# Five loads of E issued by GpSimd, the end of the cosine on VectorE, and the identity on the sync queue

## The chip, the cores and the metric

The kernel runs on one core of a Trainium2 chip. The core has a matrix engine (TensorE, PE in the profile, with its weight loads as PEld), a vector engine (VectorE, DVE), a scalar engine (ScalarE, ACT), GpSimd (POOL) and a sync engine (SP) that only issues DMAs. Each engine runs its own instructions in order and waits on semaphores for the others. SP, ACT and POOL can all issue DMAs. The metric is the device time of one execution in microseconds, the median over several runs. Less is better.

## What is computed

Two layers act on the same normalised input, and their results are added to it: a state-space convolution (`_A_ref`) and a gated feed-forward layer (`_B_ref`).

Between K and the return stands a causal convolution y of each channel of u with K, by FFT over 4096 points.

```python
def _A_ref(u, A_re, A_im, B_re, B_im, C_re, C_im, log_dt, Dskip):
    dt = jnp.exp(log_dt)[:, None]
    logdA = dt * (A_re + 1j * A_im)
    dB = dt * (B_re + 1j * B_im)
    P = jnp.exp(logdA[:, :, None] * l[None, None, :])     # l = 0 .. 2047
    K = jnp.einsum("dn,dnl,dn->dl", Cc, P, dB).real
    ...
    return y + u * Dskip[None, None, :]

def _B_ref(x, w_gate, w_up, w_down):
    h = _sigmoid(x @ w_gate) * (x @ w_up)
    return h @ w_down

x = A_u                                                    # 1 x 2048 x 512, bf16
xn = _layernorm(x, axis=-1)
return x + _A_ref(xn, ...) + _B_ref(xn, w_gate, w_up, w_down)
```

## The kernel before, in words

The convolution is done with a factored Fourier transform whose parts are matrix products. First the parameters are turned into `exp(dt*A)`, as a real and an imaginary part: its magnitude comes from an exponential, its angle from a sine and a cosine. The angle, reduced to turns, is in `w0`. ACT computes `sh`, the sine of half the angle, and `sn`, the sine of the angle, and then squares `sh` and scales it to 1 - 2 `sh`², which is the cosine (`f_sin`, L620 to L624). DVE multiplies both by the magnitude (`f_w0`, L631 and L632). From there a ladder of eleven squarings (L666 on ACT, L673 and L675 on DVE) gives the powers 1, 2, 4 and so on up to 1024, and complex products of these (`cmul`, L734 to L740, and `squares`, L789 to L795) fill two tables of powers, G and H. The product of G and H on PE (L820) gives the convolution kernel K, which goes through DRAM (`k_scr`) into the layout `kT`.

The second stage of the transform runs over two halves of the channels, p = 0 and p = 1, and over 8 units u in each, in the order that `UNITS` gives. For each unit:

- L881 transforms the unit's part of the input on PE, and ACT or DVE evicts it into `xx`. A copy with its halves of partitions swapped is made beside it, for p = 0 and for the units of `SWD` by four swap DMAs of 32 partitions on SP (`big<-big 32x1024`), else by four copies on DVE (L894).
- L907 transforms K by the constant table E of the unit: 320 KB, `es` in the code and `big<-c_E` in the profile. It is ten matmuls, evicted into `kb` by ACT.
- DVE multiplies the two spectra (L912 and L916), and L931 on PE transforms the product back. The result is evicted and stored in DRAM (`v_scr`).

The tables E have three buffers (pool `es`). In the first half all 8 are loaded; those of the units 4, 6 and 7 (`SHARED`) stay in their buffers for the second half, so that the second half loads five. A load waits until the matmuls that last read its buffer are done. PE works on the second half's units as: two kept ones, the third kept one, and then the five loaded ones. L907, L881 and L931 of all units share two PSUM pairs (pool `s`).

The feed-forward layer fills PE in between: gate (L1042), up (L1067) and down (L1119) products in four groups of 512 tokens, with sigmoids on ACT (L1055, L1058), copies of the up product on ACT (L1082), and products on DVE (L1087, L1092). What it needs of the input is normalised by L537 to L549. The first four tiles of 128 tokens are transposed on PE with the identity (`ident`, L559); the others go through DRAM. At the end L993 adds the last stage of the transform, L1017 and L1139 on DVE add everything up, and the result is stored.

The order of all work is written out by hand. Each operation gets a number in the order in which the code adds it, with an engine; `ORDER` lists the numbers, and each engine executes its operations in that order. So an operation's place in its engine's queue is its place in `ORDER`, whatever engine it has. Ahead of everything else SP loads the first four x tiles (128 KB each), then parameters and weights; ACT loads the identity, behind a small operation (`o_held`, L459) that runs after ACT's first table load. GpSimd (POOL) does small arithmetic and, late, six loads of x that are accumulated into SBUF (`facc`, L1156, 256 KB each). All other DMAs stand in SP's queue, but for a few on ACT.

Of the kernel before, what the change touches and what calls it, by code (L numbers as in the profile page):

```python
# [69 lines left out]
KB = 1024  # L70
# [114 lines left out]
def _consts():  # L185
# [136 lines left out]
def kernel(  # L322
# [116 lines left out]
    def load(q, dst, src, nbytes, deps=(), pkt=2048, hv=0.5):  # L439
        lp[0] += 0.01  # L440
        return dma(q, dst, src, deps=deps, prio=lp[0], pkt=pkt, hv=hv)(nbytes)
# [767 lines left out]
```

## Time and profile before

| what | time |
|---|---|
| median of 3 runs | 213.71 us (213.4 to 214.21) |
| time of the profiled execution | 215.62 us |
| its span, first to last instruction | 213.8 us |
| PE busy | 204.4 us (96%) |
| DVE busy | 195.5 us (91%) |
| ACT busy | 171.5 us (80%) |
| POOL busy | 16.8 us (8%) |

The profile is one execution. A timeline row gives start, duration, engine, line of the kernel, operation, what it writes and reads with shapes, how many instructions are merged in it, and in square brackets how long the engine stood idle before it and what ended that. An engine name with q (SPq, POOLq) is its sequencer or its DMA issues. A windows row gives each engine's busy time in a stretch, the granted PE clock in it, the share of the time that the 16 DMA engines were busy, and their GB/s. A chain row gives start, duration and what worked; the next row in time is what it released. Durations overlap a little: two equal DVE rows of 0.68 us can follow each other by 0.60.

### The profile page before, as it was taken

The numbers are of one execution on the slowest core, as the hardware profiler recorded it, in microseconds if no ns is written. First come the engines' busy times: TensorE is split into PE (matmuls) and PEld (weight loads), VectorE is DVE, ScalarE is ACT, GpSimd is POOL, SyncE is SP. The second block draws the span as 40 slices with busy tenths as digits, with TensorE's granted clock in tenths as the row PEclk, the third lists the DMA queues.
The fourth block names the chain that finished last, engine by engine and source line by source line (L and its number), as shares of the span: only waits on it lengthen the run. The fifth ranks groups of instructions, "written<-read, shape, count | busy, mean of one in ns | idle before, by whom it ended". The sixth has DMA issues, their size and how long they took to land.

```text
span 213.8 us, 4897 instructions
## 1 busy us (share of the span) xinstructions
PE 204.4 (96%) x1856; PEld 102.4 (48%) x1856; DVE 195.5 (91%) x412; ACT 171.5 (80%) x274; POOL 16.8 (8%) x30
## 2 busy tenths in 40 slices
PE   7898999999999999999999999999999979999992
PEld 2653444444444454445437464544653636644571
DVE  3889999999999999999999999999997979994583
ACT  3599999999999999988799998877968777891000
POOL 1003006200820000110000000011000000000000
PEclk9999999999999999999999999999999999999998
DMA  5999379101791457897575778787585569989644
GB/s 169 310 395 364 126 171 311 55 6 38 244 165 46 147 167 249 202 208 189 115 219 143 218 208 251 196 237 156 126 224 161 145 188 321 312 236 296 213 172 172
DMA packets 51465, 42.07 MB, mean 197 GB/s; under 512 B 16545, under 2 KB 44978, under 8 KB 51250
## 3 DMA queue, kind: packets, MB, share of 16 engines
q1 hardware_dynamic: 49650, 39.72, 61.7%
q0 software_dynamic: 864, 1.57, 5.1%
q10 hardware_dynamic: 928, 0.47, 0.8%
q8 instruction: 14, 0.23, 0.4%
q14 instruction: 9, 0.07, 0.1%
HBM read 24.44 MB, written 12.85 MB: 174 GB/s over the span
## 4 chain that ended last, share of the span: by engine, by line
DVE 61%; PE 20%; DMA 6%; ACT 5%; issue 4%; SPq 1%; DVEq 0%; ACTq 0%
DVE big L735 10%; DVE big L734 10%; DVE big L740 5%; DVE big L739 5%; PE bank L1119 4%; DVE hT_sb L1087 4%; PE bank L1042 4%; PE pair L931 3%; DVE big L673 3%; DVE big L675 3%; DVE big L912 3%; PE pair L907 3%; DVE hT_sb L1092 3%; PE bank L1067 3%; DVE stats L537 2%
## 5 line engine op out<-in xcount | busy, mean ns | idle before, releaser
L291 ACT ACTIVATE big<-pair 128x1024 bf16<-128x1024 f32 x62 | 64.3, 1065 | 9.1 <-PE pair L881 1.7
L1067 PE MATMUL bank<-xnT,wu_sb 128*128 128x512 bf16 x224 | 53.6, 379 | 0.1
L1119 PE MATMUL bank<-wd_sb,hT_sb 128*128 128x512 bf16 (+1 forms) x238 | 50.4, 367 | 0.0
L1042 PE MATMUL bank<-xnT,wg_sb 128*128 128x512 bf16 (+1 forms) x200 | 46.8, 371 | 1.0 <-ACT hT_sb L1055 0.9
L1042 PEld LDWEIGHTS <-wg_sb 128*128 128x128 bf16 x240 | 22.4, 98 | 26.1 <-issue 4.7
L1119 PEld LDWEIGHTS <-hT_sb 128*128 128x128 bf16 x238 | 22.5, 98 | 25.0 <-issue 1.6
L1067 PEld LDWEIGHTS <-wu_sb 128*128 128x128 bf16 x224 | 20.9, 98 | 25.0 <-issue 2.9
L1055 ACT ACTIVATE hT_sb<-bank 128x512 bf16<-128x512 f32 x48 | 29.2, 682 | 0.4 <-PE bank L1042 0.4
L734 DVE TENSOR_TENSOR big<-big 128x1024 bf16<-128x1024 bf16 (+4 forms) x40 | 26.7, 668 | 0.1
L1082 ACT ACTIVATE us_sb<-bank 128x512 bf16<-128x512 f32 x40 | 26.0, 680 | 0.9 <-DVE hT_sb L1087 0.7
L735 DVE TENSOR_TENSOR big<-big 128x1024 bf16<-128x1024 bf16 (+4 forms) x40 | 26.6, 665 | 0.0
L907 PE MATMUL pair<-big 128*128 128x256 bf16 x160 | 19.5, 273 | 2.1 <-DMA big<-c_E 1.5
L912 DVE TENSOR_TENSOR big<-big 128x2048 bf16<-128x2048 bf16 x16 | 19.5, 1220 | 1.2 <-DMA big<-big 1.1
L907 PEld LDWEIGHTS <-big 128*128 128x128 bf16 x160 | 15.3, 98 | 6.8 <-DMA big<-c_E 1.8
L789 ACT ACTIVATE sq_sb<-big 128x256 bf16<-128x256 bf16 (+2 forms) x20 | 14.4, 722 | 3.7 <-DVE big L740 3.3
L739 DVE TENSOR_TENSOR big<-big 128x512 bf16<-128x512 bf16 (+4 forms) x40 | 16.5, 412 | 0.1
L740 DVE TENSOR_TENSOR big<-big 128x512 bf16<-128x512 bf16 (+4 forms) x40 | 16.5, 412 | 0.0
L1087 DVE TENSOR_TENSOR hT_sb<-hT_sb,us_sb 128x1024 bf16<-128x1024 bf16 x20 | 13.6, 680 | 0.0
L666 ACT ACTIVATE big<-big 128x1024 f32<-128x1024 f32 x11 | 13.3, 1211 | 0.0
L931 PE MATMUL pair<-big 64*64 64x512 bf16 (+1 forms) x256 | 13.1, 327 | 0.1
L660 ACT ACTIVATE big<-big 128x512 bf16<-128x512 f32 x20 | 12.7, 754 | 0.0
L291 ACT ACTIVATE big<-big 128x256 bf16<-128x256 bf16 x25 | 11.2, 510 | 0.5 <-PE pair L820 0.5
(99 smaller groups left out, 216.8 us busy)
## 6 DMA issues: line engine op xcount, KB each, us to landing
big<-c_E SPq DMA_DIRECT2D x13, 320.0 KB, 4.1
z_scr<-big SPq DMA_DIRECT2D x16, 256.0 KB, 3.5
big<-z_scr SPq DMA_DIRECT2D x16, 256.0 KB, 3.9
v_scr<-big SPq DMA_DIRECT2D x16, 256.0 KB, 3.8
big<-big SPq DMA_DIRECT2D x44, 64.0 KB, 2.7
wu_sb<-in_B_w_up_dram SPq DMA_DIRECT2D x2, 896.0 KB, 9.4
wd_sb<-in_B_w_down_dram SPq DMA_DIRECT2D x1, 1792.0 KB, 9.9
out_dram<-big SPq DMA_DIRECT2D x7, 256.0 KB, 2.2
```

The costliest lines, as they stand in the source:

```text
L291: nc.scalar.activation(out=get(out), in_=get(in_), func=ACT.Identity)
L734: V.tensor_tensor(out=wide(outp), in0=wide(lo), in1=mre, op=ALU.mult)
L735: V.tensor_tensor(out=wide(tb()), in0=wide(lo), in1=mim, op=ALU.mult)
L739: V.tensor_tensor(out=outp[:, :, 0], in0=outp[:, :, 0], in1=tb()[:, :, 1], op=opr)
L740: V.tensor_tensor(out=outp[:, :, 1], in0=outp[:, :, 1], in1=tb()[:, :, 0], op=opi)
L907: T.matmul(two(sk)[:, o:o + DW], es()[:, g, kt, :], kTv[p][:, :, kt, :], start=kt in (0, NKT - 1), stop=kt >= NKT - 2)
L912: V.tensor_tensor(out=pp().rearrange("p q h m -> p (q h) m"), in0=xx().rearrange("p q h m -> p (q h) m"), in1=kb()[:, 0:2 * DW].unsqueeze( ...
L1042: T.matmul(bank(sl, k % 2)[:, c0:c1], w[:, kt, k * 128:(k + 1) * 128], xnT[:, grp, kt, c0:c1], start=(kt == 0), stop=(kt == KT - 1))
L1055: S.activation(out=hT_sb[:, hs.idx, k % 2, :], in_=bank(sl), func=ACT.Sigmoid)
L1067: T.matmul(bank(sl), wu_sb[:, kt, k * 128:(k + 1) * 128], xnT[:, grp, kt, :], start=(kt == 0), stop=(kt == KT - 1))
L1082: eus.append(pl.add("ACT", 0.48, lambda sl=sl, us=us, kk=kk: S.activation(out=us_sb[:, us.idx, kk % 2, :], in_=bank(sl), func=ACT.Identity ...
L1119: T.matmul(bank(po)[:, 0:c[1] - c[0]], hT_sb[:, hts[k // 2].idx, k % 2, jj * 128:(jj + 1) * 128], wd_sb[:, k, c[0]:c[1]], start=first and ...
```

## The change

It has three parts.

The identity is loaded by SP, third in its queue, behind the second x tile. `o_held` is gone, so ACT has neither that operation nor the DMA. The first rows of SP's queue, as a difference (each row is a run of equal DMAs):

```order
-L1205 UNCONDITIONAL_BRANCH
-L430 DMA big<-in_A_u_dram 128x512 x4
+L1207 UNCONDITIONAL_BRANCH
+L430 DMA big<-in_A_u_dram 128x512 x2
+L430 DMA ident<-c_ident 128x128
+L430 DMA big<-in_A_u_dram 128x512 x2
 L430 DMA big<-in_A_par_dram 128x1536
```

Tiles 3 and 4 of x, the parameters and the weights behind them stand one DMA later.

The square and the scaling of the cosine leave ACT and become a new operation on DVE, `f_cos`. In DVE's queue, where the parameters are worked out, there stood before (statistics of the input, then `f_w0`, then the end of the statistics):

```order
L616 SCALAR_TENSOR_TENSOR big<-big 128x512
L537 BN_STATS stats<-big 128x6 x4
L631 TENSOR_TENSOR big<-big 128x512
L632 TENSOR_TENSOR big<-big 128x512
L538 BN_AGGR mvb<-stats 128x2 x2
```

With the change there stands, in the same place (the line numbers move by one or two):

```order
L615 SCALAR_TENSOR_TENSOR big<-big 128x512
L536 BN_STATS stats<-big 128x6 x4
L625 TENSOR_TENSOR big<-big 128x512
L626 TENSOR_SCALAR big<-big 128x512
L633 TENSOR_TENSOR big<-big 128x512
L634 TENSOR_TENSOR big<-big 128x512
L537 BN_AGGR mvb<-stats 128x2 x2
```

L625 and L626 are new, between the statistics and `f_w0`.

The five loads of E of the second half are issued by GpSimd instead of SP. SP's queue in that part of the program, as a difference (swaps, small loads, stores and reloads stand around them):

```order
 L430 DMA big<-big 32x1024
 L430 DMA big<-in_A_u_dram 4x512
-L430 DMA big<-c_E 128x1280
 L430 DMA big<-big 32x1024 x2
-L430 DMA big<-c_E 128x1280
 L430 DMA xnT<-v_scr_101 128x2048
-L430 DMA big<-c_E 128x1280
 L430 DMA v_scr_104<-big 128x4x256
-L430 DMA big<-c_E 128x1280
```

The fifth stood further down, behind the next two stores and a reload. GpSimd's queue at its end is now, behind two fills of a table:

```order
L771 MEMSET big 128x64x2
L1158 DMA glu_sb<-in_A_u_dram 128x1024 x4
L1158 DMA big<-in_A_u_dram 128x1024 x2
L430 DMA big<-c_E 128x1280 x5
L1207 UNCONDITIONAL_BRANCH
```

The five follow its six accumulating loads of x and nothing follows them. Nothing else changes its place on any engine.

The diff, its table cut to the first line:

```diff
 ORDER = [
-    0, 1, 2, 3, 5, 4, 6, 16, 13, 8, 12, 15, 7, 22, 25, 27, 26, 28, 29, 35, 30, 31, 37, 32, 24, 36, 38, 39, 34, 40,
+    0, 1, 5, 2, 3, 4, 15, 12, 7, 11, 14, 6, 21, 24, 26, 25, 27, 28, 34, 29, 30, 36, 31, 23, 35, 37, 38, 33, 39, 40,
...
-    o_held = pl.add("ACT", 0.2, lambda: S.activation(out=ident[:, 127:128], in_=one[:], func=ACT.Identity), (), 0)
     l_pa = load("SP", par[:, 0:3, :], A_par[:, 0:3, :], 384 * KB, pkt=3072)
-    l_id = load("ACT", ident[:], cten["ident"].ap(), 32 * KB, deps=[o_held])
+    l_id = load("SP", ident[:], cten["ident"].ap(), 32 * KB)
...
     def f_sin():
         S.activation(out=pt_["sh"], in_=pt_["w0"], func=ACT.Sin, scale=PI_S)
         S.activation(out=pt_["sn"], in_=pt_["w0"], func=ACT.Sin, scale=2.0 * PI_S)
-        S.activation(out=pt_["sh"], in_=pt_["sh"], func=ACT.Square)
-        S.activation(out=pt_["sh"], in_=pt_["sh"], func=ACT.Identity, scale=-2.0, bias=one[:])
-    q5 = pl.add("ACT", 2.38, f_sin, [q3, q4], PR, tab="sin")
+    q5 = pl.add("ACT", 1.22, f_sin, [q3, q4], PR, tab="sin")
+
+    def f_cos():
+        V.tensor_tensor(out=pt_["sh"], in0=pt_["sh"], in1=pt_["sh"], op=ALU.mult)
+        V.tensor_scalar(out=pt_["sh"], in0=pt_["sh"], scalar1=-2.0, scalar2=1.0, op0=ALU.mult, op1=ALU.add)
+    q5b = pl.add("DVE", 1.1, f_cos, [q5], PR)
...
-    w0_op = cur_op = pl.add("DVE", 1.25, f_w0, [q5], PR)
+    w0_op = cur_op = pl.add("DVE", 1.25, f_w0, [q5b], PR)
...
-                le = dma("SP", es, cten["E"].ap()[u], deps=w_use[0], prio=QP - 0.5, acq=[esl], pkt=2560, hv=0.9)(320 * KB)
+                le = dma("POOL" if p else "SP", es, cten["E"].ap()[u], deps=w_use[0], prio=QP - 0.5, acq=[esl], pkt=2560, hv=0.9)(320 * KB)
```

28 rows, old and new, of the table ORDER are left out of this document.

## The prediction

> **What bounds the kernel now.** I read the chain that ended last first: by engine it is mostly VectorE (DVE), then TensorE (PE).
>
> ```profile
> DVE 61%; PE 20%; DMA 6%; ACT 5%; issue 4%; SPq 1%; DVEq 0%; ACTq 0%
> ```
>
> Then the busy times by stretch, cut where the chain changes hands.
>
> ```profile
> core 0: us, PE busy (x) PEld busy (x) DVE busy (x) ACT busy (x) POOL busy (x), PEclk, DMA share, GB/s
> 20.00:150.00 130.00, 129.76 (x1134) 60.80 (x1132) 129.44 (x296) 122.31 (x207) 13.98 (x18) 1.00 0.63 171
> 165.00:175.00 10.00, 7.97 (x70) 4.66 (x69) 8.28 (x16) 8.23 (x10) 0.00 (x0) 1.00 0.56 141
> 175.00:193.00 18.00, 17.92 (x192) 10.17 (x191) 17.72 (x31) 14.47 (x18) 0.00 (x0) 1.00 0.93 289
> ```
>
> The reader is to see three things. From 20 to 150 us PE and DVE are both full: PE has 0.24 us of idle time in 130, DVE 0.56. From 165 to 175 us nobody is full: PE stands still for 2.03 of 10 us. From 175 to 193 us PE and DVE are full again. So a microsecond counts if it is added to or taken from DVE before 150 us, or taken from the hole at 165 to 175 us.
>
> Which of the two full engines leads at 150 us is told by the chain there, in order of time:
>
> ```profile
> 148.46 0.36 DVE big L740
> ...
> 149.46 1.01 ACT big L291
> ...
> 150.51 2.34 PE pair L907 x20
> ```
>
> DVE releases an ACT copy, which releases PE's matmuls of L907. PE in turn is only just idle there, so the two lead almost together, and DVE by a hair. What keeps the hole open is a load of the table E:
>
> ```profile
> 169.84 4.58 DMA big<-c_E
> ...
> 174.47 1.27 PE pair L907 x10
> ```
>
> **The sine and cosine: ACT to DVE.** ACT now does table load, two sines, a square and a scaling in a row. These are its rows from the timeline, with start, duration, line and operation:
>
> ```profile
> 12.40 0.63 ACT L621 ACTIVATE big<-big 128x512 f32<-128x512 f32 x1
> 12.94 0.61 ACT L622 ACTIVATE big<-big 128x512 f32<-128x512 f32 x1
> 13.46 0.61 ACT L623 ACTIVATE big<-big 128x512 f32<-128x512 f32 x1
> 14.10 0.72 ACT L624 ACTIVATE big<-big,one 128x512 f32<-128x512 f32 x1
> 14.84 1.28 ACT L1055 ACT_TABLE_LOAD   x1
> ```
>
> L623 and L624 go, so the sigmoid's table load can start at about 13.5 instead of 14.84: ACT is ahead by 1.3 us. DVE's side of the same place:
>
> ```profile
> 10.51 0.43 DVE L615 TENSOR_SCALAR big<-big 128x512 f32<-128x512 f32 x1
> ...
> 11.84 2.47 DVE L537 BATCH_NORM_STATS2 stats<-big 128x6 f32<-128x512 bf16 x4 [0.18 <-DMA big<-in_A_u_dram]
> ...
> 14.86 0.69 DVE L631 TENSOR_TENSOR big<-big 128x512 f32<-128x512 f32 x1 [0.55 <-ACT big L624]
> ```
>
> DVE finishes four statistics at 14.31 and then waits 0.55 us for ACT. The new square is a tensor-tensor of the shape of L631 (0.69 us), the new scaling a tensor-scalar of the shape of L615 (0.43 us). The first sine is ready at 13.0, so DVE starts the square at 14.31 without waiting. It ends at 15.00, the scaling at about 15.45, and L631 starts at about 15.47 instead of 14.86. **That is 0.6 us more on DVE**, 1.1 us of work less 0.5 us of wait that it fills. Of this up to 0.56 us can be swallowed in the idle time that DVE has between 20 and 150 us, if that idle time is spent waiting for ACT or PE, which run earlier now. It is many pieces of a few hundredths, so I take 0.1 us of it: **+0.5 us at 150 us**, with bounds 0 and +0.6. What ACT gains, and the wait of PE for the first sigmoid, are costed at nothing: DVE releases PE at 150.5 us however far ahead PE is.
>
> **The identity on the sync queue.** Before, it waits behind ACT's first table load:
>
> ```profile
> 0.73 1.82 SPq L430 DMA_DIRECT2D big<-in_A_u_dram  x4
> ...
> 5.60 0.74 DVE L549 TENSOR_SCALAR big<-big,mv,ln_ri_f 128x512 bf16<-128x512 bf16 x2
> ...
> 6.57 0.90 PE L559 MATMUL pair<-ident,big 128*128 128x128 bf16 x8 [0.66 <-DMA ident<-c_ident]
> ...
> 8.20 0.42 PEld L1042 LDWEIGHTS <-wg_sb 128*128 128x128 bf16 x4 [0.36 <-DMA wg_sb<-in_B_w_gate_dram]
> ```
>
> An issue on SP costs 0.45 us (1.82 over 4), so the identity is issued at about 1.64 instead of 2.26 and no longer ends the wait. But L559 also needs the scaled x, which ends at 6.34, so at most 0.2 us is won there. Against it, x tiles 3 and 4, the parameters and the first weights are issued 0.45 us later. PE's next step waits for weights that land at about 8.2, and the same bytes stand in the queue ahead of them as before, so I expect no shift from the bytes; if issue time decides, it is 0.45 us. DVE's four statistics at 11.84 wait for a load too, so nothing won before reaches 14.31. I take 0, with bounds -0.2 and +0.45.
>
> **The five E loads on GpSimd.** PE's rows in the hole:
>
> ```profile
> 166.15 2.36 PE L907 MATMUL pair<-big 128*128 128x256 bf16 x20 [0.56 <-ACT big L291]
> ...
> 169.65 1.27 PE L907 MATMUL pair<-big 128*128 128x256 bf16 x10
> ...
> 172.59 0.41 PE L881 MATMUL pair<-big,m 64*64 64x512 bf16 x4
> 174.47 1.27 PE L907 MATMUL pair<-big 128*128 128x256 bf16 x10 [1.47 <-DMA big<-c_E]
> ```
>
> There are three E buffers. The first of the five loads reuses the one that the first half of the row at 166.15 reads, free at about 167.4 (ten matmuls take 1.27). SP issues the load only at 169.84, because swaps, small loads and two stores stand ahead of it in its queue. GpSimd has nothing in its queue after its last accumulating load, which is the nearest row for its price:
>
> ```profile
> 147.65 0.87 POOL L1156 DMA_DIRECT2D big<-in_A_u_dram  x1 [4.57 <-ACT big L291]
> ...
> L1156 POOL DMA_DIRECT2D glu_sb<-in_A_u_dram x4: 866/970/1209, 57.9 to 94.3; - x4
> ...
> DMA to landing us min/median/max: 4.2/5.0/5.5
> ```
>
> Those are 256 KB loads; the E load has 320 KB, another 0.2 us at the 289 GB/s of the windows row. From 167.4 it lands at 167.4 + 5.0 + 0.2 = 172.6, bounds 171.8 and 173.1. PE is ready for it at 173.0, so the wait of 1.47 us goes. Loads two and three come free at 168.6 and 170.9 and land about 174 and 176, ahead of their matmuls; four and five are freed by the matmuls of one and two and keep the distance they have now.
>
> What is late next is DVE, with ACT between:
>
> ```profile
> 173.23 0.69 DVE L916 TENSOR_TENSOR big<-big 128x1024 bf16<-128x1024 bf16 x1
> 173.97 0.59 ACT L1082 ACTIVATE us_sb<-bank 128x512 bf16<-128x512 f32 x1
> ...
> 174.99 1.22 DVE L912 TENSOR_TENSOR big<-big 128x2048 bf16<-128x2048 bf16 x1 [1.07 <-DMA big<-big]
> 175.82 1.94 ACT L291 ACTIVATE big<-pair 128x1024 bf16<-128x1024 f32 x2 [1.26 <-issue]
> ...
> 176.88 1.23 DVE L912 TENSOR_TENSOR big<-big 128x2048 bf16<-128x2048 bf16 x1
> ```
>
> The L912 at 176.88 is the product that uses E load one. From there DVE is full to 193 us, so **its start is what the tail gains**. With L907 at 173.0 to 174.2, ACT evicts at 174.5 to 175.45. But before it DVE has another L912, held 1.07 us by a swap on SP:
>
> ```profile
> 170.26 2.71 SPq L430 DMA_DIRECT2D big<-big  x2
> ```
>
> These two swaps stand right behind the E load. Without it the pair moves up by about 0.4 us and has 320 KB less ahead of it in its queue, which at 289 GB/s is 1.1 us; I take a landing at 174.0 instead of 174.95. Then the first L912 runs 173.95 to 175.1, L916 to 175.75, and the second L912 starts at 175.75 instead of 176.88: **-1.1 us**. Bounds: -1.47 if DVE takes no part, -0.1 if the swap lands no earlier (then L912 starts at 176.8).
>
> One rule speaks against GpSimd here. Row first: the copies beside which the first load would be issued.
>
> ```profile
> 166.73 1.71 DVE L894 COPY big<-big 32x1024 bf16<-32x1024 bf16 x4
> ```
>
> GpSimd's 0.87 us at 147.65 lay beside tensor-tensor work on DVE, never beside such copies. If the issue waits for the copies to end at 168.44, load one lands at 173.65, its eviction ends at 175.95, and the tail gains 0.9 instead of 1.1 us. The Trainium skill, page "SBUF — State Buffer", section "SBUF: two separate sides", says just this: a DMA issued by GpSimd has its descriptors written through ports that a DVE copy in a two-port mode locks for its whole duration. By that rule the sum is -0.4 instead of -0.6; no run here shows it yet.
>
> **Sum.** +0.5 (cosine on DVE) + 0 (identity) - 1.1 (E loads) = **-0.6 us**. The durations come from the profiled execution, whose span is 213.8 us and whose time is 215.62; there the sum gives a span of 213.2. The median of the unprofiled runs is 213.71, so I predict **213.1 us**.
>
> **Rivals.**
> First, DVE doesn't pay (212.4 us). If the 0.56 us of DVE's idle time before 150 us is mostly waiting for ACT or PE, ACT's 1.3 us of lead fills it and the front costs 0; the tail gives between 1.1 and 1.47, say 1.3. For it: PE is as full as DVE. Against it: the chain runs along DVE, and the idle time is in crumbs.
> Second, the swap takes the place of the E load (214.0 us). PE gets its table in time, but DVE still waits for the swap until near 175, and the tail gains 0.2 only; with +0.5 in front that is +0.3. For it: a swap of 64 KB waited long although it is small. Against: it stood behind the load that moves away.
> Third, slower: GpSimd is held by DVE (215.1 us). One GpSimd instruction shows how far it can be stretched (the last row is PE's use of loads four and five):
>
> ```profile
> 33.93 0.29 POOL L497 TENSOR_SCALAR ln_ve_b<-mvb 128x4 bf16<-128x4 bf16 x1 [14.20 <-DVE mvb L538]
> 53.73 2.41 POOL L497 TENSOR_SCALAR ln_ve_b<-mvb 128x4 bf16<-128x4 bf16 x1 [14.70 <-DVE mvb L538]
> ...
> 184.53 2.35 PE L907 MATMUL pair<-big 128*128 128x256 bf16 x20
> ```
>
> The same instruction takes 2.1 us more with a busy DVE. If each E load's 0.87 us becomes 3.0, the five queue up on GpSimd: issued at 167.4, 170.4, 173.4, 176.4 and 179.4, each landing 7.3 us on. Load one lands at 174.7 (174.42 now), load five at 186.7, and PE needs it at 185.8 now (the second half of the row at 184.53). That is +0.9 behind +0.5. It decides once a load takes GpSimd about 1.5 us more than 0.87. Against it: its six DMA issues took 0.87 to 1.2 us.
> That the change does not do what it says I exclude: the buffer of load one is free 2.4 us before SP issues it.
>
> **How the numbers follow.** Forecast 0.50 (212.6 to 213.6), first rival 0.20, second 0.18, third 0.12. The range 212.2 to 214.5 leaves out most of the third and a little of the first. A measurement of this kernel tells about 0.5% (1.07 us) from no change: faster than 212.64 takes 0.18 of the first rival and 0.10 of the forecast, 0.28; slower than 214.78 takes 0.11 of the third and 0.01 of the second, 0.12; the rest is 0.60.
>
> **What would show it.** In the profile after: DVE's square right behind the four statistics, no wait for ACT there, and the product behind the cosine 0.6 us later than 14.86; L907 at "150.51" about 0.5 us later; the first E load issued on GpSimd within 0.5 us of the end of its buffer's matmuls, and no PE wait for c_E; the wait of L912 for the swap gone or halved. The prediction is wrong if L907 at 150.5 doesn't move by 0.3 to 0.7, if GpSimd's issues take over 1.5 us, or if DVE's stretch from that L912 to 193 us isn't full any more.

## The result, and the profile after

| | before | after |
|---|---|---|
| median, 6 runs each | 214.14 us (213.4 to 216.95) | 215.99 us (215.06 to 217.12) |
| ratio, 95% interval | | 1.0074 [1.0046, 1.0102] |
| the profiled execution: span, time | 213.8, 215.62 us | 214.1, 215.85 us |

The change makes the kernel **slower**, by 1.6 us (0.0074 of 214). The forecast was 0.6 us faster, and 215.99 lies outside its range. The medians in this document are over all runs; the ratios, and what is worked out further down of scatter and of the share of each part, leave out executions in the chip's slower state (here the 216.95 us of the kernel before). Yet the two profiled executions differ by only 0.23 us. Both facts have to be explained, and two executions can't do it: the one before was late for its kind, as the experiments show.

First the lines of the profile after that answer to those shown of before. Line numbers are two higher behind the new `f_cos` (L909 was L907, L914 was L912) and one lower ahead of it. The shares of the chain that ended last, by engine:

```profile
DVE 66%; PE 18%; issue 6%; DMA 4%; ACT 3%; SPq 1%; DVEq 0%; ACTq 0%
```

DVE has more of it than before (61%). The stretches, with the columns of the table before:

```profile
20.00:150.00 130.00, 129.41 (x1129) 60.38 (x1128) 129.44 (x296) 121.88 (x206) 14.28 (x19) 1.00 0.62 172
...
165.00:175.00 10.00, 9.87 (x94) 5.63 (x91) 8.79 (x16) 9.15 (x11) 2.06 (x4) 1.00 0.73 201
175.00:193.00 18.00, 16.52 (x171) 9.37 (x168) 17.28 (x30) 13.59 (x18) 0.72 (x2) 1.00 0.83 256
```

DVE is as full as before from 20 to 150 us. PE's hole at 165 to 175 us is closed (9.87 instead of 7.97), and reopened behind it: from 175 to 193 us PE works 16.52 us instead of 17.92. The front, from the timeline of DVE, ACT and PE:

```profile
14.21 0.67 DVE L625 TENSOR_TENSOR big<-big 128x512 f32<-128x512 f32 x1
14.92 0.43 DVE L626 TENSOR_SCALAR big<-big 128x512 f32<-128x512 f32 x1
15.38 0.69 DVE L633 TENSOR_TENSOR big<-big 128x512 f32<-128x512 f32 x1
```

```profile
13.78 1.28 ACT L1057 ACT_TABLE_LOAD   x1
```

```profile
8.51 0.61 PE L1044 MATMUL bank<-xnT,wg_sb 128*128 128x256 bf16 x4 [0.79 <-DMA wg_sb<-in_B_w_gate_dram]
```

The square and the scaling stand right behind the statistics without a wait, the product behind them starts 0.52 us later than 14.86, ACT's table load 1.06 us earlier than 14.84, and PE's first gate matmuls 0.2 us later than 8.30. Now PE at 150 us and in the hole, by the chain of waits and then by the timeline:

```profile
150.98 2.34 PE pair L909 x20
...
166.18 2.36 PE pair L909 x20
```

```profile
173.07 1.26 PE L909 MATMUL pair<-big 128*128 128x256 bf16 x10
```

At 150 us everything is 0.47 us late (150.51 before), at 166 us only 0.03 (166.15), and the matmuls of E load one at 173.07 have lost their wait of 1.47 us and start 1.40 us earlier. GpSimd's and SP's rows of the timeline at that place:

```profile
167.75 0.58 POOL L430 DMA_DIRECT2D big<-c_E  x1 [18.74 <-PE pair L909]
168.84 0.56 POOL L430 DMA_DIRECT2D big<-c_E  x1 [0.51 <-PE pair L909]
```

```profile
167.43 0.92 SPq L430 DMA_DIRECT2D v_scr<-big  x2
...
169.70 1.48 SPq L430 DMA_DIRECT2D big<-big  x2
```

Up to here the E loads do what was forecast. What follows doesn't:

```profile
175.50 1.22 DVE L914 TENSOR_TENSOR big<-big 128x2048 bf16<-128x2048 bf16 x1 [1.49 <-ACT big L291]
176.64 0.69 DVE L918 TENSOR_TENSOR big<-big 128x1024 bf16<-128x1024 bf16 x1
177.25 1.22 DVE L914 TENSOR_TENSOR big<-big 128x2048 bf16<-128x2048 bf16 x1
```

DVE waits 1.49 us where it waited 1.07, and its product of E load one starts at 177.25 instead of 176.88. The profile names ACT as releaser, but by the landings in the trace the second of the two swaps of 169.70 came in at 175.38, just ahead of 175.50 (before: issued at 170.84, landed at 174.81). The swap was issued earlier and landed later. The DMA view shows why. Between 169.5 and 171.2 us, by queue (packets, MB, share of the 16 engines), first of before, then of after:

```profile
q1 hardware_dynamic: 429, 0.28, 74.9%
```

```profile
q0 software_dynamic: 54, 0.28, 84.0%
q1 hardware_dynamic: 29, 0.01, 2.9%
issues: line engine op xcount, KB each, median us to landing
big<-big SPq DMA_DIRECT2D x2, 64.0 KB, 5.4
```

q0 is GpSimd's queue, q1 SP's. In after GpSimd's E load holds 84% of the engines, and SP's queue, with the store and the swaps, moves 29 packets where it moved 429 (11 of these were of its own E load). By the landings, the second `v_scr` store, issued at 167.90, took 5.7 us instead of 2.8.

### The profile page after: what moved, and what is told of

Read it like the earlier page. It is cut to its first block, busy times and chain, and to the rows that moved or that the text cites. A ratio compares the mean times of both kernels' runs of the same rounds, so it can differ in the third digit from the quotient of the medians.

```text
span 214.1 us, 4899 instructions
## 1 busy us (share of the span) xinstructions
PE 205.1 (96%) x1856; PEld 102.0 (48%) x1856; DVE 196.4 (92%) x414; ACT 170.4 (80%) x271; POOL 19.6 (9%) x35
## 3 DMA queue, kind: packets, MB, share of 16 engines
q0 software_dynamic: 1264, 3.21, 7.3%
## 4 chain that ended last, share of the span: by engine, by line
DVE 66%; PE 18%; issue 6%; DMA 4%; ACT 3%; SPq 1%; DVEq 0%; ACTq 0%
DVE big L737 10%; DVE big L736 10%; DVE big L742 5%; DVE big L741 5%; PE bank L1121 4%; PE bank L1044 4%; DVE big L914 4%; DVE hT_sb L1089 4%; DVE stats L536 3%; DVE big L675 3%; DVE big L677 3%; DVE hT_sb L1094 3%; PE pair L909 3%; ACT big L291 2%; DMA wg_sb<-in_B_w_gate_dram 2%
## 5 line engine op out<-in xcount | busy, mean ns | idle before, releaser
L291 ACT ACTIVATE big<-pair 128x1024 bf16<-128x1024 f32 x62 | 62.6, 1036 | 9.5 <-DVE big L918 3.6
L1069 PE MATMUL bank<-xnT,wu_sb 128*128 128x512 bf16 x224 | 54.3, 379 | 0.4 <-ACT hT_sb L1057 0.3
L1057 ACT ACTIVATE hT_sb<-bank 128x512 bf16<-128x512 f32 x48 | 27.2, 615 | 0.3 <-PE bank L1044 0.3
L1084 ACT ACTIVATE us_sb<-bank 128x512 bf16<-128x512 f32 x40 | 24.0, 620 | 0.5 <-DVE hT_sb L1089 0.2
L914 DVE TENSOR_TENSOR big<-big 128x2048 bf16<-128x2048 bf16 x16 | 19.5, 1218 | 1.6 <-ACT big L291 1.5
L909 PE MATMUL pair<-big 128*128 128x256 bf16 x160 | 19.5, 273 | 0.2
L909 PEld LDWEIGHTS <-big 128*128 128x128 bf16 x160 | 15.3, 98 | 4.9 <-issue 0.7
L791 ACT ACTIVATE sq_sb<-big 128x256 bf16<-128x256 bf16 (+2 forms) x20 | 13.4, 671 | 3.9 <-DVE big L742 3.6
L668 ACT ACTIVATE big<-big 128x1024 f32<-128x1024 f32 x11 | 11.9, 1086 | 0.3 <-DVE big L677 0.3
L662 ACT ACTIVATE big<-big 128x512 bf16<-128x512 f32 x20 | 11.7, 649 | 0.0
L536 DVE BATCH_NORM_STATS2 stats<-big 128x6 f32<-128x512 bf16 x12 | 7.8, 684 | 3.6 <-DMA big<-in_A_u_dram 3.6
```

The lines of the kernel that those rows point to most:

```text
L291: nc.scalar.activation(out=get(out), in_=get(in_), func=ACT.Identity)
L909: T.matmul(two(sk)[:, o:o + DW], es()[:, g, kt, :], kTv[p][:, :, kt, :], start=kt in (0, NKT - 1), stop=kt >= NKT - 2)
L914: V.tensor_tensor(out=pp().rearrange("p q h m -> p (q h) m"), in0=xx().rearrange("p q h m -> p (q h) m"), in1=kb()[:, 0:2 * DW].unsqueeze( ...
L1057: S.activation(out=hT_sb[:, hs.idx, k % 2, :], in_=bank(sl), func=ACT.Sigmoid)
L1069: T.matmul(bank(sl), wu_sb[:, kt, k * 128:(k + 1) * 128], xnT[:, grp, kt, :], start=(kt == 0), stop=(kt == KT - 1))
L1084: eus.append(pl.add("ACT", 0.48, lambda sl=sl, us=us, kk=kk: S.activation(out=us_sb[:, us.idx, kk % 2, :], in_=bank(sl), func=ACT.Identity ...
```

## The experiments

**A ruler.** Six DVE rows cut the span into pieces. In the profile before they are the first statistics (3.44 us), the product behind the cosine (14.86), the L1092 at 157.18, L842 behind the load from `k_scr` (165.82), the L916 at 173.23, the L912 with E load one (176.88) and the last L1139 (209.92). The same instructions were read, start to start, in every profile that follows. "x tile" is from the first statistics to the four statistics ahead of the cosine; they wait for a load of x. "60 PE instructions", "cold" and "warm" are explained with e10 and e13.

| kernel | x tile | to the product behind the cosine | to L1092 | to L842 | to L916 | to the product of E load one | to the end |
|---|---|---|---|---|---|---|---|
| before | 8.40 | 11.42 | 142.32 | 8.63 | 7.42 | 3.64 | 33.05 |
| e2, E loads | 8.96 | 11.40 | 142.26 | 8.16 | 7.47 | 3.35 | 33.04 |
| e3, cosine | 9.07 | 12.63 | 142.23 | 8.13 | 7.41 | 2.86 | 33.03 |
| e4, identity | 9.34 | 11.73 | 142.21 | 8.71 | 7.42 | 4.14 | 33.04 |
| e6, cosine, identity | 9.03 | 12.58 | 142.23 | 8.25 | 7.41 | 4.30 | 33.05 |
| e7, identity, E loads | 9.04 | 11.43 | 142.31 | 8.15 | 7.47 | 2.35 | 33.03 |
| e8, cosine, E loads | 9.33 | 12.88 | 142.21 | 8.21 | 7.47 | 3.88 | 33.09 |
| after | 8.41 | 11.97 | 142.27 | 8.19 | 7.47 | 3.93 | 33.04 |
| e9, first load only | 8.45 | 11.39 | 142.29 | 8.24 | 7.46 | 3.19 | 33.04 |
| e17, the same again | 8.69 | 11.43 | 142.29 | 8.13 | 7.45 | 2.54 | 33.04 |
| e18, cosine, identity, first load | 8.71 | 12.27 | 142.26 | 8.13 | 7.46 | 2.81 | 33.03 |
| e11, cosine with one operation | 8.56 | 11.66 | 142.26 | 8.13 | 7.41 | 2.60 | 33.04 |
| e10, 60 PE instructions (cold) | 9.41 | 12.67 | 142.30 | 8.26 | 7.41 | 2.34 | 33.67 |
| e12, the same, E loads | 8.79 | 12.04 | 142.32 | 8.25 | 7.46 | 2.35 | 33.04 |
| e13, 60 PE instructions (warm) | 9.12 | 11.51 | 142.29 | 8.25 | 7.41 | 2.35 | 33.04 |
| e14, the same, whole change | 8.95 | 12.51 | 142.26 | 8.28 | 7.46 | 2.34 | 33.50 |
| e15, the same, cosine | 8.97 | 12.53 | 142.26 | 8.24 | 7.41 | 2.34 | 33.35 |
| e16, the same, E loads | 8.40 | 11.68 | 142.27 | 8.30 | 7.46 | 2.34 | 33.04 |

Three columns are rigid within 0.15 us, but for the last one of e10, e14 and e15: whatever DVE is late at 15 us, it is late at 157 us. Nearly all the difference lies in three places: the front, the wait for `k_scr`, and the way from L916 to E load one. What the ruler leaves out is its own start: the first statistics start at 2.91 to 3.44 us.

**e1: the kernel before, again.** No edit.

> The kernel before, once more. Its first profile has a span of 213.8 us and a time of 215.62, while its unprofiled runs lie at 213.4 to 214.2; the changed kernel's runs all lie 1.8 us above their spans. Theory A: that one profile was an odd, slower execution; then this profile's span is 212.0 to 212.6, and ACT's evictions take less (L1055 and L1058 nearer 615 ns than 682). Theory B: a profile of this kernel always shows 213.8, and the gap lies outside the span. The ratio to itself is 1.000, within 0.2%, by both.

Measured: 214.19 us median, ratio 0.998 [0.9949, 1.0011]. The execution that was profiled took 418.55 us, with PE at little over half its usual speed (L1067's matmuls took 674 ns instead of 379), so it answers nothing on the profile; the same happened in e5 (530.1 us), and both profiles are left out below. A second execution of e5 took 264.06 us and one of the kernel before 596.62, without a profile. But five groups of runs of the kernel before, 150 executions, have a median of 214.53 us and 8 in 10 of them between 213.54 and 215.52. So 213.71, the median of three, was a lucky draw, and 215.62, the profiled one, lay near the slow end: theory A, as far as times can show it.

**e2, e3, e4: each part alone.** The five loads:

```diff
-                le = dma("SP", es, cten["E"].ap()[u], ...)
+                le = dma("POOL" if p else "SP", es, cten["E"].ap()[u], ...)
```

> Only the five E loads go to GpSimd. Theory 'sharing' (the loads start 2 us earlier and their bytes hold back the swaps and the store that SP issues at 168 to 171): the last two swaps land 0.5 to 1 us later than in the control, the product of E load one starts no earlier, and the kernel is slower by 0.4 to 1.6 us (ratio 1.002 to 1.0075). Rival 'front' (the loss comes from the cosine and the identity): ratio 0.995 to 1.001. Third (my forecast's tail): faster by 1.1 us, ratio 0.995.

Measured: 215.05 us, ratio 0.9996 [0.9967, 1.0025]. My gain of 1.1 us is excluded, and so is most of the loss that 'sharing' had; its small end, 1.002, is not. Alone the loads do nothing that these runs can tell.

The cosine:

```diff
-        S.activation(out=pt_["sh"], in_=pt_["sh"], func=ACT.Square)
-        S.activation(out=pt_["sh"], in_=pt_["sh"], func=ACT.Identity, scale=-2.0, bias=one[:])
...
+    def f_cos():
+        V.tensor_tensor(out=pt_["sh"], in0=pt_["sh"], in1=pt_["sh"], op=ALU.mult)
+        V.tensor_scalar(out=pt_["sh"], in0=pt_["sh"], scalar1=-2.0, scalar2=1.0, op0=ALU.mult, op1=ALU.add)
...
```

> Only the square and the scaling go to DVE. Theory 'front': DVE pays 0.5 us at the product behind the cosine and this arrives at the end: ratio 1.002 to 1.003. Theory 'absorbed': the 0.5 us is there at 150 us and gone by 166 us, where PE and DVE wait for the convolution kernel's way through DRAM: ratio 1.000 within 0.1%.

Measured: 215.29 us, ratio 1.0014 [0.998, 1.0048]; the interval allows both. The timeline of DVE doesn't:

```profile
12.00 2.47 DVE L537 BATCH_NORM_STATS2 stats<-big 128x6 f32<-128x512 bf16 x4 [0.80 <-DMA big<-in_A_u_dram]
14.39 0.67 DVE L626 TENSOR_TENSOR big<-big 128x512 f32<-128x512 f32 x1
15.09 0.43 DVE L627 TENSOR_SCALAR big<-big 128x512 f32<-128x512 f32 x1
15.55 0.69 DVE L634 TENSOR_TENSOR big<-big 128x512 f32<-128x512 f32 x1
```

DVE's wait is now ahead of the statistics, for the load of x; the sine is ready long before 14.39. The front takes 12.63 us, and nothing of it is absorbed by 157 us (142.23).

The identity:

```diff
-    o_held = pl.add("ACT", 0.2, lambda: S.activation(out=ident[:, 127:128], in_=one[:], func=ACT.Identity), (), 0)
-    l_id = load("ACT", ident[:], cten["ident"].ap(), 32 * KB, deps=[o_held])
+    l_id = load("SP", ident[:], cten["ident"].ap(), 32 * KB)
```

> Only the identity goes to SP. Theory 'issue time': everything behind it on SP is issued 0.45 us later, PE's first gate matmuls start 0.2 to 0.45 us later and the end moves by as much: ratio 1.001 to 1.002. Rival 'hidden': the first gate matmuls move by 0.2 us but DVE's four statistics at 11.8 us don't, and the ratio is 1.000 within 0.1%.

Measured: 215.32 us, ratio 1.003 [1.0, 1.006]; the interval holds 'issue time' and just reaches 'hidden'. Its front is 11.73 us, 0.3 more than in before and e2, and the timeline of DVE says that the load of x came late, though no later than in e8 (9.33 us), whose identity is on ACT:

```profile
12.29 2.47 DVE L536 BATCH_NORM_STATS2 stats<-big 128x6 f32<-128x512 bf16 x4 [0.88 <-DMA big<-in_A_u_dram]
14.68 0.67 DVE L630 TENSOR_TENSOR big<-big 128x512 f32<-128x512 f32 x1
```

**e5 to e8: the whole, and the whole without one part.** e5 is the change as it is; e6 has SP issue the E loads again, e7 has the cosine back on ACT, e8 the identity.

```diff
e6
-                le = dma("POOL" if p else "SP", es, ...)
+                le = dma("SP", es, ...)
e7
...
-    q5b = pl.add("DVE", 1.1, f_cos, [q5], PR)
...
+        S.activation(out=pt_["sh"], in_=pt_["sh"], func=ACT.Square)
+        S.activation(out=pt_["sh"], in_=pt_["sh"], func=ACT.Identity, scale=-2.0, bias=one[:])
...
e8
...
-    l_id = load("SP", ident[:], cten["ident"].ap(), 32 * KB)
+    l_id = load("ACT", ident[:], cten["ident"].ap(), 32 * KB, deps=[o_held])
```

> The whole change once more, with more runs. In the first four runs the parts alone cost -0.1 (E loads), +0.3 (cosine) and +0.5 us (identity), each give or take 0.7. Theory 'the parts add up': +0.7 us, ratio 1.003. Rival 'they need each other' (the E loads collide with SP's transfers only when the front is late): +1.6 us, ratio 1.0075.

> The change without its E loads: cosine on DVE and identity on SP only. 'The parts add up': +0.7 us, ratio 1.003, the same as the whole within 0.3 us. Rival 'they need each other': less than the whole by 0.8 us or more.

> The change without the cosine: identity on SP and E loads on GpSimd. 'The parts add up': +0.45 us, ratio 1.002; DVE's product behind the cosine stands 0.2 to 0.3 us later than with the E loads alone, because PE's first gate weights land later and hold a copy on DVE that stands ahead of the sines. If the identity costs nothing in front: ratio 1.000.

> The change without the identity: cosine on DVE and E loads on GpSimd. 'The parts add up': +0.2 us, ratio 1.001. If the identity is what costs: at or below the kernel before. If the cosine costs its full 0.5 us at the end and the E loads give nothing back: ratio 1.0025 to 1.003.

| run | median, us | ratio, 95% interval |
|---|---|---|
| e5, whole | 216.95 | 1.0092 [1.0056, 1.0128] |
| e6, without the E loads | 215.98 | 1.0061 [1.0027, 1.0096] |
| e7, without the cosine | 215.06 | 1.0017 [0.9983, 1.005] |
| e8, without the identity | 215.72 | 1.0059 [1.0031, 1.0087] |

e5 is larger than 'the parts add up' had it from the first four runs, but the parts had errors of 0.7 us each. e8 is slower than it had it too (1.001), and e6's interval just holds its 1.003. The cosine is the largest: only e7, without it, comes near the kernel before. The E loads win nothing in e5 against e6 either, and e8 shows the collision of the section above once more: its second store was issued at 168.18, just behind GpSimd's load at 168.13, and took 4.8 us by the landings. In e2 and e7 the store was issued 0.64 and 0.82 us ahead of the load, landed in 3.1 us, and from L916 to E load one it takes 3.35 and 2.35 us, against 3.88 and 3.93 in e8 and after. With the first load alone on GpSimd (next) the same shows in e17 (store 0.62 us ahead, 2.8 us) and e9 (0.19 us behind, 4.8 us), less in e18 (0.12 us behind, 3.4 us).

**e9, e17, e18: only the first load on GpSimd.** If the second load, issued a microsecond behind the first, is what the swaps have to share the engines with, it should stay in SP's queue behind them. In the kernel before (e9, and again e17):

```diff
-                le = dma("SP", es, ...)
+                le = dma("POOL" if p and u == 5 else "SP", es, ...)
```

> Of the five E loads only the first goes to GpSimd; the four others stay in SP's queue, behind the swaps. Theory 'the loads get in the way of the swaps': in every profile with all five loads on GpSimd the last two swaps landed 3.4 to 5.4 us after their issue, beside load one and two; with load two back behind them they land within 3.5 us, DVE's product of load one starts 3.4 us or less after the product before it (2.4 to 4.3 in the profiles so far), and the kernel is 0.3 to 1 us faster than before, ratio 0.995 to 0.9985. Rival 'it is chance' (the place is set by where PE's instruction fetches fall): ratio 1.000.

> Only the first E load on GpSimd, once more. If 0.3% was no luck: ratio 0.994 to 0.999 again, faster than before by 0.3 to 1.2 us, with a spread below 0.5 us. If it was luck of one session: ratio 1.000, spread 0.9 us as in the kernel before.

Measured: **213.75 us, ratio 0.9967 [0.9944, 0.999]**, and again **213.73 us, 0.9962 [0.9936, 0.9988]**. This version beats both kernels. Its standard deviation is 0.32 and 0.39 us over 12 executions each; before it is 0.75 over 150. DVE in e9:

```profile
172.31 0.69 DVE L916 TENSOR_TENSOR big<-big 128x1024 bf16<-128x1024 bf16 x1
173.76 1.23 DVE L912 TENSOR_TENSOR big<-big 128x2048 bf16<-128x2048 bf16 x1 [0.75 <-DMA big<-big]
174.90 0.69 DVE L916 TENSOR_TENSOR big<-big 128x1024 bf16<-128x1024 bf16 x1
175.50 1.22 DVE L912 TENSOR_TENSOR big<-big 128x2048 bf16<-128x2048 bf16 x1
```

Its wait for the swap is 0.75 us. My expectation that the swaps land within 3.5 us of their issue failed: they took 4.0 to 4.7 us in e9 and 4.1 to 4.4 in e17, against 5.0 to 5.4 in after. But with all five loads on GpSimd they took 4.4 to 4.5 us in e7, and in before, with none, 4.0 and 4.4. So the profiles do not show that the second load is what holds them. In e9 another cause is seen: 15 of the 16 engines had landed their parts of the two swaps by 172.18 and 172.34 us, the last one at 173.42 and 173.63, with a packet of PE instructions (see e10 below) at 171.18; in e2 it was 172.72 and 173.72, with a packet at 171.43. That the first load alone wins is shown by the times; by what way, these profiles leave open.

e18 puts the same edit into the changed kernel:

> The whole change, but of the E loads only the first on GpSimd. If four of the five loads are what the change loses in the tail: 0.6 to 1.1 us faster than the whole change (ratio to before 1.001 to 1.003, the cosine's and the identity's part left over). If cosine and identity alone make the loss and the loads' place doesn't matter: ratio 1.005 to 1.008.

Measured: 215.18 us, ratio 1.0027 [0.9997, 1.0056]; from L916 to E load one 2.81 us instead of 3.93. By the ratios it is faster than the whole change by 1.0 us (first measurement) to 1.4 (e5), as the first theory had it, though the interval reaches to the rival's 1.005; it is still not faster than before.

**e10, e12, e13 to e16: PE's instruction fetch.** The way from L916 to E load one varies by 1.4 us between e3 and e6, in which nothing that differs stands near it. The DMA view of before, between 169.8 and 171.5 us, while load one is issued and under way, shows a packet of another kind:

```profile
q1 hardware_dynamic: 267, 0.21, 68.3%
q8 instruction: 1, 0.02, 6.8%
issues: line engine op xcount, KB each, median us to landing
big<-c_E SPq DMA_DIRECT2D x1, 320.0 KB, 4.6
```

There are 14 such packets of 16384 bytes in the profile, from the first to the last on average one for 254 PE instructions, weight loads counted. In the trace this one occupies one of the 16 DMA engines from 170.84 for 1.85 us, and of the E load 15 engines' parts landed by 173.04 and the last at 174.42. The first of the two swaps behind it shows the same (15 parts by 173.22, the last at 174.62). In e4 and e6, where the way is longest, the packet takes 2.05 and 2.37 us and the last part is 1.9 and 1.8 us late. The Trainium skill, page "Runtime: NRT & Kernel Launch", section "Instruction fetch mechanics", says that an engine's program is fetched in blocks of 16 KiB, 256 instructions, over a DMA queue, at a cost "mostly hidden"; the size agrees with the trace, and the cost here isn't hidden.

To move the fetch, PE got 60 more instructions ahead of everything. In e10 forty warming matmuls of 64 columns took the place of ten of 512 ("cold": they end early, and PE's next matmuls run slowly), in e13 forty of 128 ("warm"). The first packet of this kind moves from 21.65 us in before to 13.22 in e13, so these are PE's:

```diff
-    def keep_warm(n, prio):
+    def keep_warm(n, prio, cols=512):
-                T.matmul(bank(wsl), glu_sb[:, 0, 0:128], glu_sb[:, 0, :], start=True, stop=True)
+                T.matmul(bank(wsl)[:, 0:cols], glu_sb[:, 0, 0:128], glu_sb[:, 0, 0:cols], start=True, stop=True)
-    keep_warm(10, -10)
+    keep_warm(40, -10, 64)        (e10, e12; 128 in e13 to e16)
```

e12 adds the E loads on GpSimd to e10; e14, e15 and e16 add the whole change, the cosine and the E loads to e13.

> The kernel before, but PE's ten warming matmuls of 512 columns at the start are forty of 64, so that PE has 60 more instructions ahead of everything and its 16 KB instruction fetches, at 159 and 171 us in the profile before, come some 60 instructions earlier, at 155 to 156 and 167 to 169 us. Theory 'fetch': then the last part of the k_scr stores lands within 0.8 us of the others (1.8 us before), the wait for k_scr on DVE is 8.1 us rather than 8.6 counted from the product before it, the first E load lands 2.9 to 3.2 us after its issue (4.6 before), and the kernel is 0.5 to 1.5 us faster, ratio 0.993 to 0.998. Rival 'fetch is harmless': nothing moves, ratio 1.000. If the warming matters, PE is slower before 20 us and the ratio is over 1.

> The sixty more PE instructions together with the five E loads on GpSimd. Theory 'fetch': with the fetch out of the way SP's loads of E are no longer late, so GpSimd's have less to win: within 0.3 us of the run with the shift alone, ratio 0.993 to 0.998. Theory 'the loads get in the way of the swaps': 0.3 to 0.8 us slower than the shift alone. My forecast's tail: 0.7 to 1.1 us faster than the shift alone.

> The kernel before with the 60 more PE instructions at the start, this time as forty warming matmuls of 128 columns, which together last as long as the ten of 512, so that PE stays warm. Theory 'fetch': the front is back at 11.4 us from the first statistics to the product behind the cosine (12.7 with 64 columns), DVE's wait for the swap is 0.6 us again, its product of load one starts 2.35 us after the product before it, and the kernel is 0.7 to 1.5 us faster than before with a spread below 0.5 us, ratio 0.993 to 0.997. Rival 'the 64 columns only shifted DVE against the loads': the wait is 1.5 to 2 us again and the ratio 1.000.

> The whole change with the same 60 more PE instructions. If the cosine costs 1.1 us of DVE time, the identity 0.2, and the E loads nothing once the fetch is away: 1.3 us slower than the kernel before with the 60 instructions. If the E loads still hold back the swaps: 1.6 to 2.5 us slower.

> The cosine alone with the 60 more PE instructions: 1.1 us slower than the kernel before with them ('DVE pays everything it is given'), or 0.5 (my forecast, which took half of it for filled waiting). From the first statistics to the product behind the cosine: 12.5 to 12.9 us against 11.4.

> The five E loads alone with the 60 more PE instructions: within 0.2 us of the kernel before with them, if what the loads win on SP (1.3 us of waiting) is already gone with the fetch; 0.3 to 1 us slower if the loads still hold back the store and the swaps; 1.1 us faster by my forecast.

| run | median, us | ratio, 95% interval |
|---|---|---|
| e10, 60 instructions (cold) | 215.32 | 1.0053 [1.0028, 1.0078] |
| e12, the same, E loads | 215.21 | 1.0032 [1.0006, 1.0058] |
| e13, 60 instructions (warm) | 214.52 | 0.9996 [0.9969, 1.0023] |
| e14, the same, whole change | 215.39 | 1.0051 [1.0024, 1.0078] |
| e15, the same, cosine | 214.87 | 1.0014 [0.9986, 1.0042] |
| e16, the same, E loads | 214.31 | 0.9997 [0.9968, 1.0026] |

At the place itself the theory holds in six of six profiles. The fetch has gone to 165 to 166 us (in e13 it is in the stretch from 164 to 167):

```profile
q8 instruction: 1, 0.02, 2.1%
```

The E load lands 3.0 us after its issue, still on SP (from 167.5 to 169 us):

```profile
big<-c_E SPq DMA_DIRECT2D x1, 320.0 KB, 3.0
```

And DVE and PE have no hole left, in the stretch from 165 to 175 us of e13 and in its DVE rows:

```profile
165.00:175.00 10.00, 9.96 (x94) 5.79 (x93) 9.78 (x18) 9.19 (x11) 0.00 (x0) 1.00 0.82 246
```

```profile
172.45 0.69 DVE L916 TENSOR_TENSOR big<-big 128x1024 bf16<-128x1024 bf16 x1
173.06 1.22 DVE L912 TENSOR_TENSOR big<-big 128x2048 bf16<-128x2048 bf16 x1
174.19 0.69 DVE L916 TENSOR_TENSOR big<-big 128x1024 bf16<-128x1024 bf16 x1
174.79 1.22 DVE L912 TENSOR_TENSOR big<-big 128x2048 bf16<-128x2048 bf16 x1
```

The way is 2.34 to 2.35 us in all six, whether SP or GpSimd issues the loads. That is the lowest seen, a floor 1.3 us below the profile before.

In the times the theory fails. e10 pays 1.3 us in front, by PE's timeline because the short matmuls end early, PE stands idle for 2.07 us and the next ones run slowly (0.53 us for 512 columns, 0.26 in e13):

```profile
5.84 1.01 PE L559 MATMUL pair<-ident,big 128*128 128x128 bf16 x8 [2.07 <-DVE big L549]
...
7.51 1.06 PE L524 MATMUL bank<-glu_sb 128*128 128x512 bf16 x2 [0.22 <-issue]
```

e13 repairs the front (11.51), but its median is the kernel's before, and its deviation 0.73 us, not below 0.5. e14, e15 and e10 show a new loss of 0.3 to 0.6 us at the end. Where the typical execution of e13 loses what its profile wins, no profile here shows; that stays open. So the fetch is shown to lengthen the wait at 171 to 175 us, and not shown to make the spread of the whole. It is not the only way to the floor either: e7 takes 2.35 us with its fetch at 171.60, when load one (landed at 171.38) was already in.

Within this group the E loads are worth nothing (e16 against e13, 214.31 and 214.52 us; e12 against e10, 215.21 and 215.32), the whole change costs 0.9 us, the cosine 0.35 by medians and 1.0 in the front of the profiles.

**e11: the cosine on DVE with one operation instead of two.**

```diff
+        V.scalar_tensor_tensor(out=pt_["sh"], in0=pt_["sh"], scalar=-2.0, in1=pt_["sh"], op0=ALU.mult, op1=ALU.mult)
-        V.tensor_tensor(out=wt[0][:, 0, :], in0=pt_["rr"], in1=pt_["sh"], op=ALU.mult)
+        V.scalar_tensor_tensor(out=wt[0][:, 0, :], in0=pt_["sh"], scalar=1.0, in1=pt_["rr"], op0=ALU.add, op1=ALU.mult)
```

> The cosine on DVE alone, at half its price: one added operation (minus two times the square, 0.69 us) and the scaling folded into the product with the magnitude. Theory 'DVE pays everything it is given': from the first statistics to that product it takes 0.5 us less than with two operations (12.0 to 12.4 us instead of 12.6 to 12.9; 11.4 without any), and the whole is 0.5 to 0.6 us slower than before, ratio 1.0025. Rival 'DVE's idle time takes it': ratio 1.000.

Measured: 215.08 us, ratio 1.0017 [0.9983, 1.0051]. The front took 11.66 us, less than expected, because the x tile came early (8.56); from the four statistics to the product it is 3.10 us, against 3.56 with two operations in all seven profiles, and 2.39 where neither ACT nor a further operation stands between (e4, e7, e13). DVE pays each operation in full: 0.71 and 0.46.

## Why the prediction was wrong

**All parts together.** A least-squares sum of parts over the 347 executions of all kernels but e10 and e12 (e11 counted as half a cosine, the 60 instructions as a term of their own, -0.3 ± 0.13) gives, with standard errors: cosine +0.8 ± 0.11 us, identity +0.5 ± 0.12, five E loads +0.3 ± 0.12, first load alone -0.8 ± 0.14, on a base of 214.5. The three parts add up to 1.6 us; 1.6 were measured. The sum takes the parts as independent. With a term for each pair of parts, identity and E loads together cost 0.6 ± 0.24 us less than their sum, so the identity's share is the least certain.

**The base.** "The median of the unprofiled runs is 213.71" was right and too few: the kernel scatters by a microsecond, and three runs happened to be early. That moves the forecast in us by 0.8, not its sign.

**The cosine: right mechanism, half the size.** The step that failed is "1.1 us of work less 0.5 us of wait that it fills". The wait of 0.55 us is what is left when the x tile comes early. Of the eight profiles with the cosine on ACT and PE warm, four have such a wait (before, e9, e16 and e17, tile at 8.40 to 8.69), and four have none to speak of (e2, e4, e7 and e13, 8.96 to 9.34). With ACT the front is 11.4 to 11.7 us either way, because the load of x and ACT's chain end almost together; with DVE it is the tile's arrival plus 3.56 us, 12.0 to 12.9. The means of the table are 11.50 (8 profiles, PE warm) and 12.48 (7): **+1.0 us, not +0.5**. In after's profile the tile was early (8.41), which is why it showed the +0.47 at 150 us that I had forecast: that agreement was luck. That DVE's idle time takes hardly any of it, and that ACT's lead of a microsecond is worth nothing, was right.

Between 150 and 166 us the profile pair hides the loss: before waits 8.63 us to L842, after 8.19. Of the 18 profiles only before and e4 are above 8.30, so this is a chance of before's profile and no gain of the change. In the trace of before, too, the last part of the `k_scr` stores landed 1.8 to 2 us behind the other 15, with an instruction packet at 159 us.

**The identity: outside its bounds, or at their end.** I took 0 with +0.45 as the worst. The times say +0.5 ± 0.12. The profiles show a part: the gate weights land later, and a copy on DVE ahead of the sines with them (DVE's L616, or its counterpart, starts 7.77 us after the first statistics in e4, 7.88 in e6 and 7.78 in after, though 7.57 in e7; 7.49 to 7.57 in before, e2, e3 and e8). That is up to 0.3 us where ACT's chain sets the front. Another part lies ahead of the ruler: in the six profiles with the identity on SP the first statistics, which wait for the first load of x, start at 2.95 to 3.41 us, on average 3.21; in the twelve with it on ACT at 2.91 to 2.99 in ten and 3.43 and 3.44 in two, on average 3.02. So what failed is "I take 0": as far as these profiles show, the loads of x and of the weights beside the identity came later. The rest is not located, and whether the issue time of the one DMA ahead makes it, as my upper bound had it, wasn't tried.

**The E loads: the wait went, the gain didn't.** PE's wait of 1.47 us vanished as forecast, load one was issued at 167.75 and landed at 173.02 (forecast 167.4 and 172.6). The step that failed is "has 320 KB less ahead of it in its queue, which at 289 GB/s is 1.1 us; I take a landing at 174.0". The load left SP's queue, but not the 16 engines behind it; issued earlier, it and the second load stood in front of the store and the swaps, and the swap landed at 175.38. That is the second rival, "the swap takes the place of the E load", at a chance of 0.18; but its gain of 0.2 us lies four standard errors from the times (a loss of 0.3 ± 0.12), and its 214.0 was too little because the base, the cosine and the identity were too. The Trainium skill has the rule I should have weighed, page "DMA: Bandwidth & Descriptors", section "Issuing engines are not separate DMA queues": DMAs run on the same 16 engines whoever issues them, and another issuer saves only issue time. The trace agrees, and goes further: the other queue's packets fell from 429 to 29 in 1.7 us.

**The rivals.** The first (DVE doesn't pay) is excluded by the rigid 142.2 to 142.3 us from the product behind the cosine to L1092. The third (GpSimd held by DVE) didn't happen: the issues took 0.55 to 0.58 us, the first of them beside DVE's copies from 166.76 to 168.56. The sum of -0.4 by the Trainium skill's rule on the shared ports, "SBUF: two separate sides" on the page "SBUF — State Buffer", needed an issue held until the copies ended; no run here shows one. By the trace of after the first packets of load one came 1.77 us after its issue; those of the accumulating loads at 142.70 and 148.14 us, with no such copy beside them, took 2.00 and 1.57. Only in e18 they came later, after 2.85 us, and why stays open.

## What to carry to other kernels

Take the size of a wait that new work is to fill from several executions: a wait between two engines that finish almost together can be there in one execution and gone in the next. Where one engine was full, work given to it was paid in full, and time won on an engine that wasn't was worth nothing. A transfer moved to another issuer still meets the same engines; ask which small transfers it will now stand in front of, and move only the one that something waits for: one load on GpSimd won 0.7 to 0.8 us where five won nothing (0.3 us lost, in the sum of parts).

## What was unexpected

A fetch of PE instructions can delay a load without PE's waiting for the instructions: a 16384-byte packet on one of 16 DMA engines held that engine's share of a load back by 1.4 to 1.9 us (before, e4, e6), and the matmuls waited until the last share was in (174.42 us in before; they start at 174.47). Moving it by 60 PE instructions took 1.3 us out of that place in six profiles of six, and nothing that can be told out of the median (e13, ratio 0.9996).

GpSimd's E loads went out in packets of 5120 bytes, SP's in 2560, counted from the trace; between 169.5 and 171.2 us, while load one ran in after, 29 of SP's 512-byte packets (the store) went out, against 347 in before.
